# Block 0 of a fused attention and GEGLU kernel: other PSUM banks, an earlier third tile, two gates moved ahead

## The chip, the cores and the metric

The kernel runs on one core of a Trainium2 chip. The metric is the device time of one execution in microseconds; the value given for a kernel is the median of its runs. Before the change it is 328.77 us over 8 runs (328.52 to 329.89).

## What is computed

Two steps follow each other. A linear attention over 8 batches, 8 heads, 576 positions and 64 features per head; and a gated feed-forward layer on its output, seen as 4608 tokens of 512 channels, with 1536 hidden units. All tensors are float32 at the interface.

```python
r = np.maximum(x, 0.0)                        # phi of q and of k
phi = np.concatenate([r * cos_w, r * sin_w], axis=-1)
kv  = einsum('bhsf,bhsd->bhfd', phi(k), v)
num = einsum('bhsf,bhfd->bhsd', phi(q), kv)
den = einsum('bhsf,bhf->bhs', phi(q), sum_s phi(k)) + 1e-6
x   = (num / den)                             # tokens by 512 channels
g   = x @ w_gate
out = (0.5 * g * (1 + erf(g / sqrt(2))) * (x @ w_val)) @ w_out
```

## The kernel before, in words

**Work.** TensorE works in bfloat16. The tokens are cut into nine blocks: block 0 is batch 0 with its 576 tokens, and the others have 512 tokens, the last 448. A block's feed-forward part goes through the 12 groups of 128 hidden units, called `jt` in the code. `gate` (L212 to L222) multiplies one group's gate weights with the tokens in four accumulating matmuls into a PSUM bank, from which ScalarE writes the Gelu to a tile `gel`. `value` (L224 to L233) does the same with the value weights into another bank, and VectorE multiplies that bank by `gel` into `hT`. `gv_unit` is a gate and then its value. The output matmuls (L258) read `hT`.

**Banks.** One PSUM tile `ps` has 8 banks of 512 float32 columns, and every call names its bank as a number: the arguments of `gate` and `value` are block, group, first column, width and bank. Nothing is double-buffered by a pool here. A matmul into a bank waits until the last reader of that bank is done, so the numbers written in the calls decide who waits for whom. `gel` is from a rotating pool with 3 buffers.

**Order.** The order of instructions on every engine is the order of the Python calls (a manual schedule). Engines run in order, so a waiting instruction holds everything behind it on its engine.

**Block 0.** The start of the kernel cannot hide behind other work, so its calls are written out by hand (L396 to L439). The attention of batch 0 is cut into five tiles of tokens, the fifth with 64 tokens. For tile `t` these steps follow each other:

- `sq(t, which, engine)` (L134, L136) scales q by cosine or sine, on VectorE ("v") and ScalarE ("s").
- `q_by_pe(0, t, bank, engine)` (L323, L331, L333) transposes q in 8 matmuls and copies the bank to `qT`. `q_evac` is the copy alone.
- `Y(t, bank)` makes the numerators: 8 matmuls (L169), four into `bank` and four into `bank + 1`, then the division on VectorE (L181, L183, L184) into a tile `xb`.
- `X(t, bank, engine)` transposes `xb` in 4 matmuls (L342) into `bank`, and an engine copies it to `xT` (L345). Gates and values read `xT`.

As soon as a tile's columns of `xT` are there, gates and values on these columns can run. In block 0 the groups 0 and 1 are worked in pieces of 128 columns (0, 128, 256, 384) and a last one of 64 (512); later groups in A, 256 columns from 0, and Bw, 320 columns from 256. A loop (L467 to L472) then does the groups 4 to 11, with gate and value in the banks 0 and 3 for A and 1 and 2 for Bw, leaving out what the hand-written part has done.

**Queues.** The weights of the groups come by DMAs that GpSimd issues (L304, L305): groups 0 to 1, 2 to 3, 4 to 7 and later 8 to 11. Behind these in GpSimd's order stand the load of batch 1's q (L79), which may start when batch 0's q has been read, then the two halves of the output weights `wo_sb` (L443, L444), and a small copy (L445) that waits for the first half; the loads of batch 1's k and v on SyncE's queue wait for that copy.

**Dummies.** `dummies` (L123) issues matmuls on a zeroed tile `junk` at the start, while TensorE has nothing else to do.

Of the kernel before, what the change touches and what calls it, by code (L numbers as in the profile page):

```python
# [9 lines left out]
FP32 = mybir.dt.float32  # L10
BF16 = mybir.dt.bfloat16
# [5 lines left out]
def kernel(  # L17
# [31 lines left out]
    sb = ctx.enter_context(tc.tile_pool(name="sb", bufs=1))  # L49
    rot = ctx.enter_context(tc.tile_pool(name="rot", bufs=2))  # L50
# [16 lines left out]
    kv = [sb.tile([128, H, D + 2], BF16, name=f"kv{i}") for i in range(2)]  # L67

    hT = [sb.tile([128, JT, 64 + 576], BF16, name=f"hT{i}") for i in range(2)]
    ident = sb.tile([128, 128], BF16, name="ident")  # L70
    junk = sb.tile([128, 512], BF16, name="junk")
    tiny = sb.tile([1, 8], FP32, name="tiny")


# [54 lines left out]
    def scale(f, j, which, eng, h0=0, h1=H):  # L129
        dst, src = f  # L130
        col = (cos_c if which == 0 else sin_c)[:, j:j + 1]
        s, d = src[:, h0:h1, j, :], dst[:, j, h0:h1, which * D:(which + 1) * D]
        if eng == "v":
            nc.vector.tensor_scalar(d, s, col, 0.0, op0=ALU.mult, op1=ALU.max)  # L134
        else:
            nc.scalar.activation(d, s, AF.Relu, scale=col)  # L136
# [55 lines left out]
    def numer(b, t, bank, rows=128):  # L192

        numer_mm(b, t, bank, 0, rows)
        numer_mm(b, t, bank, 1, rows)
        xb = new_xb()
        norm(xb, bank, 0, 2, rows)
        return xb
# [12 lines left out]
    gels = {}  # L211

    def gate(n, jt, c0, w, gb):

        p0 = starts[n] + c0
        for ct in range(CT):
            nc.tensor.matmul(  # L217
                ps[:, gb, 0:w], lhsT=wg_sb[:, ct, jt * 128:(jt + 1) * 128],
                rhs=xT[:, ct, p0:p0 + w], start=(ct == 0), stop=(ct == CT - 1),
            )  # L220
        gels[n, jt, c0] = gel = rot.tile([128, 512], FP32, name="gel", bufs=3)
        nc.scalar.activation(gel[:, 0:w], ps[:, gb, 0:w], AF.Gelu)  # L222

    def value(n, jt, c0, w, vb):  # L224

        p0 = starts[n] + c0
        for ct in range(CT):
            nc.tensor.matmul(  # L228
                ps[:, vb, 0:w], lhsT=wv_sb[:, ct, jt * 128:(jt + 1) * 128],
                rhs=xT[:, ct, p0:p0 + w], start=(ct == 0), stop=(ct == CT - 1),  # L230
            )
        gel = gels.pop((n, jt, c0))
        nc.vector.tensor_mul(hT[n % 2][:, jt, 64 + c0:64 + c0 + w], gel[:, 0:w], ps[:, vb, 0:w])  # L233

    def gv_unit(n, jt, c0, w, gb, vb, mid=()):
        gate(n, jt, c0, w, gb)
        for f in mid:
            f()
        value(n, jt, c0, w, vb)
# [79 lines left out]
    def q_by_pe(b, j, bank, eng, h0=0, h1=H):  # L319

        qb = ps[:, bank, :].bitcast(BF16).rearrange("p (h t) -> p h t", h=H)
        for h in range(h0, h1):
            nc.tensor.transpose(out=qb[:, h, :], in_=qp[:, j, h, :], identity=ident)  # L323
        if eng is not None:
            q_evac(b, j, bank, eng, h0, h1)

    def q_evac(b, j, bank, eng, h0=0, h1=H):
        qb = ps[:, bank, :].bitcast(BF16).rearrange("p (h t) -> p h t", h=H)
        cp = nc.vector.tensor_copy if eng == "v" else nc.scalar.copy
        if j < NJ:  # L330
            cp(qT[b % 2][:, j, h0:h1], qb[:, h0:h1])  # L331
        else:
            cp(qT[b % 2][:, j, h0:h1, 0:64], qb[:, h0:h1, 0:128:2])  # L333

    def x_by_pe(b, t, xb, bank, eng, c0=0, c1=CT, every=1):
        p0 = b * S + t * 128
        cp = nc.vector.tensor_copy if eng == "v" else nc.scalar.copy
        xb2 = xb.rearrange("p g h d -> p (g h d)")
        rows = 128 if t < NJ or every == 2 else 64
        view = ps[:, bank, 0:256].bitcast(BF16).rearrange("p (c t) -> p c t", c=CT)  # L340
        for ct in range(c0, c1):
            nc.tensor.transpose(  # L342
                out=view[:, ct, 0:rows], in_=xb2[0:rows, ct * 128:(ct + 1) * 128], identity=ident[0:rows, 0:rows],
            )
        cp(xT[:, c0:c1, p0:p0 + rows // every], view[:, c0:c1, 0:rows:every])  # L345

    def sq(j, which, eng, *h):
        scale(Q, j, which, eng, *h)
# [48 lines left out]
    A, Bw = (0, 256), (256, 320)  # L397
    xs = {1: x1}

    def X(t, bank, eng):  # L400
        return lambda: x_by_pe(0, t, xs[t], bank, eng)

    def Y(t, bank):
        def f():
            xs[t] = numer(0, t, bank, 128 if t < NJ else 64)
        return f

    gate(0, 0, 0, 128, 5)
    gate(0, 1, 0, 128, 4)
    X(1, 2, "v")()  # L410
    q_evac(0, 2, 3, "v")
    sq(3, 0, "v"), sq(3, 1, "s")
    value(0, 0, 0, 128, 6)
    value(0, 1, 0, 128, 7)
    gate(0, 0, 128, 128, 5)
    gate(0, 1, 128, 128, 4)
    sq(4, 1, "s"), sq(4, 0, "v")
    value(0, 0, 128, 128, 6)
    value(0, 1, 128, 128, 7)
    Y(2, 2)()  # L420
    q_by_pe(0, 3, 0, "s")
    q_by_pe(0, 4, 1, "v")
    gv_unit(0, 2, *A, 4, 6)
    X(2, 0, "s")()
    Y(3, 2)()
    gv_unit(0, 3, *A, 5, 7)
    gv_unit(0, 0, 256, 128, 4, 6)
    X(3, 1, "v")()
    Y(4, 2)()
    gv_unit(0, 1, 256, 128, 5, 7)  # L430
    gv_unit(0, 0, 384, 128, 4, 6)
    gv_unit(0, 1, 384, 128, 5, 7)
    X(4, 0, "v")()
    gate(0, 4, *A, 3)
    gv_unit(0, 2, *Bw, 4, 6)
    gv_unit(0, 3, *Bw, 5, 7)
    value(0, 4, *A, 1)
    gv_unit(0, 0, 512, 64, 0, 2)
    gv_unit(0, 1, 512, 64, 4, 6)  # L439


    load_q(1, nc.gpsimd)
# [23 lines left out]
    }  # L466
    for jt in range(4, 12):  # L467
        for i, (c0, w) in enumerate((A, Bw)):
            if (jt, i) != (4, 0):
                gv_unit(0, jt, c0, w, i, 3 - i)  # L470
            for f in between.get((jt, i), ()):
                f()  # L472
# [52 lines left out]
    for n in range(1, 7):  # L525
# [6 lines left out]
        s = 0 if n > 1 else -1  # L532
# [68 lines left out]
```

## Time and profile before

| | |
|---|---|
| Median of 8 runs | 328.77 us |
| The profiled execution's own time | 328.52 us |
| Its span, first to last instruction | 326.4 us |
| Outside the span | 2.1 us |
| Mean granted TensorE clock | 1.000 |
| TensorE matmul busy | 316.7 us, 97% |
| VectorE busy | 172.2 us, 53% |
| ScalarE busy | 150.5 us, 46% |

In a profile line, L217 is line 217 of the kernel; PE is TensorE's matmuls, DVE is VectorE, ACT is ScalarE, POOL is GpSimd, SP is SyncE. A line of a timeline has the start, the time from the start to the end of the merged instructions, the engine, the line, the operation, `output<-inputs`, the shapes, the count, and in brackets how long the engine had been idle and what released it. Matmuls are pipelined: the next one starts well before the modelled end of the one before. So what a group of matmuls occupies is read from start to start, and an idle time in brackets, which counts from that modelled end, is shorter than the time that TensorE lost.

### The profile page before, as it was taken

What the parts mean: (1) busy time and instruction counts of PE and PEld (TensorE: products, weight loads), DVE (VectorE), ACT (ScalarE), POOL (GpSimd) and SP (SyncE); (2) the same over time, 40 slices, a digit from 0 to 9 for tenths busy, and PEclk for the clock granted to TensorE, in tenths of its full rate; (3) what the DMA queues carried; (4) which work ended last, traced back from release to release, by engine and by line L of the source; (5) the groups of instructions that cost most, each with busy time, mean ns of one, the idle gap of its engine ahead of it and who ended that gap; (6) DMA issues with size and microseconds to landing.
All of it is one profiled execution on the core that took longest, in us unless ns stands there. A gap on an engine that the chain in (4) does not pass through costs nothing.

```text
span 326.4 us, 5828 instructions
## 1 busy us (share of the span) xinstructions
PE 316.7 (97%) x2188; PEld 167.2 (51%) x2222; DVE 172.2 (53%) x383; ACT 150.5 (46%) x269; POOL 21.3 (7%) x41
## 2 busy tenths in 40 slices
PE   7999999999999999999999999999999999999994
PEld 3587866554445544544455445544554444444543
DVE  5895776868653667365835484548455222222210
ACT  6554664772483256425652375237622332323321
POOL 2640010000100010001000010001000100100000
PEclk9999999999999999999999999999999999999999
DMA  7999999896799929993799359994523211000024
GB/s 227 283 205 274 228 318 311 292 227 117 222 263 296 283 60 167 300 259 82 135 306 284 80 108 198 367 137 87 140 54 76 46 34 34 32 32 32 34 65 96
DMA packets 87739, 55.42 MB, mean 170 GB/s; under 512 B 52512, under 2 KB 82976, under 8 KB 87712
## 3 DMA queue, kind: packets, MB, share of 16 engines
q1 hardware_dynamic: 81200, 48.71, 59.7%
q0 software_dynamic: 6080, 5.90, 10.1%
q10 hardware_dynamic: 432, 0.46, 0.5%
q8 instruction: 17, 0.28, 0.4%
q14 instruction: 10, 0.08, 0.1%
HBM read 37.75 MB, written 9.44 MB: 145 GB/s over the span
## 4 chain that ended last, share of the span: by engine, by line
PE 94%; DVE 3%; issue 1%; ACT 0%; DVEq 0%
PE ps L217 28%; PE ps L258 28%; PE ps L228 27%; PE ps L169 3%; PE ps L153 3%; PE ps L126 2%; PE ps L323 1%; DVE hT L233 1%; PE ps L276 1%; PE ps L342 1%; DVE xb L184 1%; DVE vx L140 0%; DVE qp L134 0%; DVE rec L183 0%; DVE qT L331 0%
## 5 line engine op out<-in xcount | busy, mean ns | idle before, releaser
L233 DVE TENSOR_TENSOR hT<-gel,ps 128x512 bf16<-128x512 f32 (+5 forms) x126 | 76.4, 610 | 128.6 <-PE ps L228 121.8
L228 PE MATMUL ps<-xT,wv_sb 128*128 128x512 bf16 (+5 forms) x492 | 111.8, 348 | 1.1 <-DVE hT L233 0.8
L217 PE MATMUL ps<-xT,wg_sb 128*128 128x512 bf16 (+5 forms) x490 | 111.8, 348 | 1.0
L222 ACT ACTIVATE gel<-ps 128x512 f32<-128x512 f32 (+5 forms) x126 | 67.5, 536 | 77.6 <-PE ps L217 75.3
L258 PE MATMUL ps<-wo_sb,hT 128*128 128x512 bf16 x413 | 95.5, 379 | 0.6
L228 PEld LDWEIGHTS <-wv_sb 128*128 128x128 bf16 x504 | 47.9, 98 | 47.1 <-issue 1.0
L217 PEld LDWEIGHTS <-wg_sb 128*128 128x128 bf16 x504 | 45.7, 98 | 40.6 <-DVE xT L345 0.4
L258 PEld LDWEIGHTS <-hT 128*128 128x128 bf16 x420 | 40.1, 98 | 45.4
L287 ACT COPY o_sb<-ps 128x512 f32<-128x512 f32 x35 | 20.5, 585 | 75.4 <-PE ps L258 74.4
L184 DVE TENSOR_TENSOR xb<-ps,rec 128x512 bf16<-128x512 f32 (+2 forms) x41 | 27.8, 678 | 1.7 <-DVE rec L183 0.2
L136 ACT ACTIVATE kp<-kf,sin_c 128x512 bf16<-128x512 f32 (+1 forms) x41 | 25.4, 680 | 0.1
L134 DVE TENSOR_SCALAR qp<-qf,cos_c 128x512 bf16<-128x512 f32 x40 | 20.3, 547 | 0.0
L169 PEld LDWEIGHTS <-qT 128*128 128x128 bf16 (+1 forms) x320 | 15.0, 98 | 9.1 <-issue 2.3
L136 ACT ACTIVATE qp<-qf,sin_c 128x512 bf16<-128x512 f32 x28 | 19.3, 713 | 0.2 <-DMA qf<-in_q_dram 0.2
L134 DVE TENSOR_SCALAR kp<-kf,cos_c 128x512 bf16<-128x512 f32 (+1 forms) x45 | 18.6, 463 | 0.8 <-DMA kf<-in_k_dram 0.8
L169 PE MATMUL ps<-kv,qT 128*128 128x65 bf16 (+1 forms) x320 | 16.5, 193 | 0.5 <-DVE xb L184 0.3
L208 POOL COPY xT<-xr 128x256 bf16<-128x256 bf16 x6 | 2.4, 400 | 200.4 <-DMA xr<-xb 200.4
L153 PEld LDWEIGHTS <-kp 128*128 128x128 bf16 x320 | 10.9, 97 | 2.6 <-issue 0.7
L126 PE MATMUL ps<-junk 128*128 128x512 bf16 x33 | 10.1, 458 | 1.8 <-DVE par_i L103 1.7
L153 PE MATMUL ps<-vx,kp 128*128 128x65 bf16 x320 | 11.1, 193 | 0.1
L140 ACT CAST vx<-vf 128x1280 bf16<-128x1280 f32 (+1 forms) x9 | 9.7, 1075 | 1.2 <-DMA vf<-in_v_dram 1.2
L244 POOL COPY hT<-hT 128x768 bf16<-128x768 bf16 x8 | 7.6, 945 | 37.6 <-DVE hT L233 37.6
(55 smaller groups left out, 88.3 us busy)
## 6 DMA issues: line engine op xcount, KB each, us to landing
out_dram<-o_sb SPq DMA_DIRECT2D x38, 128.0 KB, 2.4
kf<-in_k_dram SPq DMA_DIRECT2D x7, 640.0 KB, 7.2
out_dram<-o_sb SPq DMA_DIRECT2D x16, 256.0 KB, 3.1
qf<-in_q_dram SPq DMA_DIRECT2D x6, 640.0 KB, 6.0
vf<-in_v_dram SPq DMA_DIRECT2D x6, 640.0 KB, 9.3
kf<-in_k_dram SPq DMA_DIRECT2D x7, 512.0 KB, 6.1
qf<-in_q_dram SPq DMA_DIRECT2D x6, 512.0 KB, 5.0
vf<-in_v_dram SPq DMA_DIRECT2D x6, 512.0 KB, 8.3
```

Of the source, the lines that this page charges most:

```text
L126: nc.tensor.matmul(ps[:, bank, :], lhsT=junk[:, 0:128], rhs=junk, start=True, stop=True)
L134: nc.vector.tensor_scalar(d, s, col, 0.0, op0=ALU.mult, op1=ALU.max)
L136: nc.scalar.activation(d, s, AF.Relu, scale=col)
L153: nc.tensor.matmul(ps[:, bank, (h % 4) * (D + 1):(h % 4 + 1) * (D + 1)], lhsT=kp[:, j, h, :], rhs=vx[b % 2][:, j, h, 0:D + 1], start=(j == ...
L169: nc.tensor.matmul(ps[0:rows, bank + g, (h % 4) * (D + 1):(h % 4 + 1) * (D + 1)], lhsT=qT[b % 2][:, t, h, 0:rows], rhs=kv[b % 2][:, h, 0:D ...
L184: nc.vector.tensor_tensor(xb[0:rows, g0:g1], nd[:, :, :, 0:D], rec[0:rows, 0:n, :, None].to_broadcast([rows, n, 4, D]), op=ALU.mult,)
L217: nc.tensor.matmul(ps[:, gb, 0:w], lhsT=wg_sb[:, ct, jt * 128:(jt + 1) * 128], rhs=xT[:, ct, p0:p0 + w], start=(ct == 0), stop=(ct == CT - 1),
L222: nc.scalar.activation(gel[:, 0:w], ps[:, gb, 0:w], AF.Gelu)
L228: nc.tensor.matmul(ps[:, vb, 0:w], lhsT=wv_sb[:, ct, jt * 128:(jt + 1) * 128], rhs=xT[:, ct, p0:p0 + w], start=(ct == 0), stop=(ct == CT - 1),
L233: nc.vector.tensor_mul(hT[n % 2][:, jt, 64 + c0:64 + c0 + w], gel[:, 0:w], ps[:, vb, 0:w])
L258: nc.tensor.matmul(ps[:, bank, :], lhsT=hT[n % 2][:, jt, c0:c0 + 128], rhs=wo_sb[:, jt, :], start=(jt == 0), stop=(jt == JT - 1),)
L287: nc.scalar.copy(o_sb, ps[:, bank, :])
```

## The change

The changed kernel keeps every computation; it reorders block 0, names other banks, and moves three copies between engines.

- **Tile of the dummies.** `junk` is no longer a tile of its own but the first 512 columns of group 0 in `hT[1]`, which is written for real in block 1.
- **Buffers.** `gel` has 4 buffers where it had 3.
- **First units.** The values of groups 0 and 1 on the columns 128 to 255 go to the banks 2 and 3 where they went to 6 and 7. The copy of `X(1, 2, ...)` goes from VectorE to ScalarE, that of `X(2, 0, ...)` from ScalarE to VectorE, that of the fourth tile from VectorE to ScalarE with bank 0 in place of 1, and the copy of the fifth tile's transposed q from VectorE to ScalarE.
- **Third tile.** `Y(2, 0)` stands right behind the first two values; it stood as `Y(2, 2)` behind the second two. All later `Y` use the banks 0 and 1.
- **Fifth tile of q.** `sq(4, ...)` and `q_by_pe(0, 4, ...)` come later.
- **Two gates ahead.** The gates of the groups 4 and 5 on A stand ahead of the last columns' units (before, that of group 4 alone), and their values behind them; the loop leaves out both.

```diff
+    junk = hT[1][:, 0, 0:512]
-    junk = sb.tile([128, 512], BF16, name="junk")
...
-        gels[n, jt, c0] = gel = rot.tile([128, 512], FP32, name="gel", bufs=3)
+        gels[n, jt, c0] = gel = rot.tile([128, 512], FP32, name="gel", bufs=4)
...
     gate(0, 0, 0, 128, 5)
     gate(0, 1, 0, 128, 4)
-    X(1, 2, "v")()
+    X(1, 2, "s")()
     q_evac(0, 2, 3, "v")
     sq(3, 0, "v"), sq(3, 1, "s")
     value(0, 0, 0, 128, 6)
     value(0, 1, 0, 128, 7)
+    Y(2, 0)()
     gate(0, 0, 128, 128, 5)
     gate(0, 1, 128, 128, 4)
+    value(0, 0, 128, 128, 2)
+    value(0, 1, 128, 128, 3)
+    q_by_pe(0, 3, 6, "s")
+    gate(0, 2, *A, 5)
+    X(2, 0, "v")()
     sq(4, 1, "s"), sq(4, 0, "v")
-    value(0, 0, 128, 128, 6)
-    value(0, 1, 128, 128, 7)
-    Y(2, 2)()
-    q_by_pe(0, 3, 0, "s")
-    q_by_pe(0, 4, 1, "v")
-    gv_unit(0, 2, *A, 4, 6)
-    X(2, 0, "s")()
-    Y(3, 2)()
-    gv_unit(0, 3, *A, 5, 7)
-    gv_unit(0, 0, 256, 128, 4, 6)
-    X(3, 1, "v")()
-    Y(4, 2)()
-    gv_unit(0, 1, 256, 128, 5, 7)
-    gv_unit(0, 0, 384, 128, 4, 6)
-    gv_unit(0, 1, 384, 128, 5, 7)
+    value(0, 2, *A, 7)
+    gate(0, 3, *A, 4)
+    Y(3, 0)()
+    value(0, 3, *A, 2)
+    q_by_pe(0, 4, 3, "s")
+    gv_unit(0, 0, 256, 128, 5, 6)
+    X(3, 0, "s")()
+    Y(4, 0)()
+    gv_unit(0, 1, 256, 128, 4, 7)
+    gv_unit(0, 0, 384, 128, 5, 2)
+    gv_unit(0, 1, 384, 128, 4, 3)
+    gate(0, 4, *A, 5)
     X(4, 0, "v")()
-    gate(0, 4, *A, 3)
-    gv_unit(0, 2, *Bw, 4, 6)
-    gv_unit(0, 3, *Bw, 5, 7)
-    value(0, 4, *A, 1)
-    gv_unit(0, 0, 512, 64, 0, 2)
-    gv_unit(0, 1, 512, 64, 4, 6)
+    gate(0, 5, *A, 4)
+    gv_unit(0, 2, *Bw, 1, 6)
+    gv_unit(0, 3, *Bw, 0, 7)
+    value(0, 4, *A, 3)
+    value(0, 5, *A, 2)
+    gv_unit(0, 0, 512, 64, 4, 6)
+    gv_unit(0, 1, 512, 64, 5, 7)
...
-            if (jt, i) != (4, 0):
+            if (jt, i) not in ((4, 0), (5, 0)):
                 gv_unit(0, jt, c0, w, i, 3 - i)
```

## The prediction

> **What bounds the kernel now.** First the page: engine shares and the chain of work that ended last.
>
> ```profile
> PE 316.7 (97%) x2188; PEld 167.2 (51%) x2222; DVE 172.2 (53%) x383; ACT 150.5 (46%) x269; POOL 21.3 (7%) x41
> ...
> PE 94%; DVE 3%; issue 1%; ACT 0%; DVEq 0%
> ```
>
> TensorE is busy 97% and makes 94% of the chain. The change keeps every matmul, so it can only win or lose TensorE's idle time in the stretch that it reorders, 16 to 31 us. Behind it, the list of TensorE's waits has one of 0.3 us after 60 us: what TensorE gains early is kept. Next, TensorE's timeline of the stretch.
>
> ```profile
> 16.27 0.61 PE L217 MATMUL ps<-xT,wg_sb 128*128 128x128 bf16 x8
> 16.85 0.40 PE L342 MATMUL ps<-ident,xb 128*128 128x128 bf16 x4
> 17.08 0.61 PE L228 MATMUL ps<-xT,wv_sb 128*128 128x128 bf16 x8
> 17.76 0.62 PE L217 MATMUL ps<-xT,wg_sb 128*128 128x128 bf16 x8
> 18.95 0.61 PE L228 MATMUL ps<-xT,wv_sb 128*128 128x128 bf16 x8 [0.56 <-DVE hT L233]
> 19.39 0.42 PE L169 MATMUL ps<-kv,qT 128*128 128x65 bf16 x8
> 19.65 1.05 PE L323 MATMUL ps<-ident,qp 128*128 128x128 bf16 x16
> 20.54 0.60 PE L217 MATMUL ps<-xT,wg_sb 128*128 128x256 bf16 x4
> 20.97 0.60 PE L228 MATMUL ps<-xT,wv_sb 128*128 128x256 bf16 x4
> ...
> 24.88 0.39 PE L217 MATMUL ps<-xT,wg_sb 128*128 128x128 bf16 x4
> 25.50 0.38 PE L228 MATMUL ps<-xT,wv_sb 128*128 128x128 bf16 x4 [0.23 <-DVE hT L233]
> ...
> 29.51 0.28 PE L228 MATMUL ps<-xT,wv_sb 128*128 128x64 bf16 x4
> 29.86 0.70 PE L217 MATMUL ps<-xT,wg_sb 128*128 128x320 bf16 x4
> ```
>
> Where nothing waits, the distance of starts gives what a matmul occupies: 16 transposes from 19.65 to 20.54, 0.056 us for 128 columns; likewise 0.109 for 256, 0.136 for 320, 0.029 for 64, and 0.033 in the numerators. A start later than that is lost time: 17.76 + 8 x 0.056 = 18.21, but the next row starts at 18.95. Last, hand-over times:
>
> ```profile
> 17.28 0.42 DVE L345 COPY xT<-ps 128x512 bf16<-128x512 bf16 x1 [0.49 <-PE ps L342]
> ...
> 20.29 1.01 ACT L331 COPY qT<-ps 128x1024 bf16<-128x1024 bf16 x1 [0.42 <-PE ps L323]
> ...
> 21.83 0.59 ACT L345 COPY xT<-ps 128x512 bf16<-128x512 bf16 x1 [0.24 <-PE ps L342]
> ```
>
> The first copy ends at 17.70 and TensorE starts at 17.76: 0.06 from engine to TensorE. The four transposes from 21.41 last 0.39 and ScalarE starts at 21.83: from the point where TensorE could go on (21.63) that is 0.16 for the pipeline and 0.04 for the hand-over. One copy of this size is 0.59 on ScalarE, 0.42 on VectorE.
>
> **What it removes.**
> - *Values on columns 128, banks 6 and 7.* Wait now 18.95 - 18.21 = 0.73: the bank is freed by a product that stands on VectorE behind the copies of xT and qT (17.28 to 18.30) and a scaling. The banks 2 and 3 are free by then. -0.73. Next late is nothing there; their products find VectorE free after the division.
> - *Value of group 1 on column 384, bank 7.* 24.88 + 0.22 = 25.10 against 25.50: 0.40. Its bank 3 was last read by the copy of the fifth q tile, which I place at 22.2 to 22.8. -0.40.
> - *First gate of the loop, bank 1.* 29.51 + 0.12 = 29.63 against 29.86: -0.24. Bank 1 is then last read by a Gelu some 2 us earlier.
> - *Gates on columns 128.* Wait now 17.08 + 0.45 = 17.53 to 17.76, 0.23. With ScalarE copying, xT comes at 17.28 + 0.59 + 0.06 = 17.93; the third tile's numerators (8 x 0.033) fill 17.53 to 17.79; 0.14 is left. -0.09. Their qT is ready: its copy, 0.68, now starts right after the division, at 16.7.
> - *Small ones.* Between the fourth tile's transposes and the fifth's numerators, which load 64 columns of weights, TensorE loses 0.09 (23.27 + 4 x 0.056 against 23.60); this falls inside a new wait. The last columns' first gate waits 0.05 for xT and will find it ready, with 0.44 of another gate ahead. Another 0.01 where the fourth tile's xb is awaited. Together -0.15.
>
> Sum removed: 0.73 + 0.40 + 0.24 + 0.09 + 0.15 = 1.61.
>
> **What it adds.** I carried every engine's new order forward with these durations. Applied to the old order, that gave TensorE's start at 32.91 within 0.02.
> - *The fifth tile's numerators now go to bank 0, into which the fourth tile has just been transposed.* TensorE must stand still for a whole copy: 0.16 + 0.04 + 0.59 + 0.06 = 0.85. No row shows this pair; the numerators write other columns and 64 partitions only. The built order has a wait on ScalarE at the first of them. [...] Everything on TensorE stands behind it. Upper end 1.1, were the copy of qT and a Gelu queued ahead on ScalarE to run late.
> - *Loop, group 5 on Bw.* Group 5 on A has gone, so groups 4 and 5 on Bw use the banks 1 and 2 in direct succession. The gate needs the Gelu (0.44, ScalarE row of 320 columns) done: 0.16 + 0.04 + 0.44 + 0.06 = 0.70 after the gate before, of which the value covers 0.54: 0.15. The value then waits for the product of 0.49 (VectorE row) with 0.11 in front: 0.82 - 0.70, 0.10 to 0.12. +0.25.
> - *The value of group 2 on A moves from 20.97 to 19.94.* Its weights, issued by GpSimd at 11.64, land 8.3 us later, and the last of the 16 parts is there at 19.99. +0.11 with the hand-over; between 0 and 0.4, since an earlier landing was never needed so exactly.
>
> Sum added: 0.85 + 0.25 + 0.11 = 1.21.
>
> **What costs nothing.** Group 5's gate and value on A (8 x 0.109 = 0.87) leave the loop and enter the hand-written part. The fourth `gel` buffer only removes ScalarE's waits (1.2 us there, which TensorE doesn't feel). The dummies read another zeroed address. Of the copies moved to ScalarE, the fifth q tile's gates nothing soon. The fifth q tile's scaling on ScalarE now comes behind a copy of 1.01 and a Gelu and ends near 21.43, not 19.87. Two things are queued on that: the transposes of q, which TensorE reaches at 21.6, cover 0.14; and GpSimd's second load of batch 1's q, issued now at 20.16 and then near 21.7, with both halves of `wo_sb` behind it (20.85, 21.66) 1.55 later. These land only 16 to 19 us after issue, because the queue ahead of them is full until 41; so I leave their landing. Were it 1.55 later, so would be batch 1's k, from 44.2 to 45.7, where ScalarE wants it at 45.55 - 0.40: 0.6 on ScalarE, of which the two output tiles (45.56 to 50.74; the features and v are ready at 50.16) cover all but 0 to 0.1.
>
> [...] By the row it is 1.61 - 1.21 = 0.40. [...]
>
> **Sum.** The profiled execution took 328.52 (span 326.4), 0.25 below the median of 328.77. 328.52 - 0.40 = 328.12 for it; for the median 328.77 - 0.40 = 328.37, so **328.4**. A measurement of this kernel tells about 0.2%, 0.66 us, from no change: bounds 328.11 and 329.43.
>
> **Rivals.**
> - *No new bank wait* (the numerators don't stand behind the copy): 0.40 + 0.85 = 1.25 gained, 327.5. For it: 64 partitions and other columns; against it: the wait in the built order. 0.10.
> - *ScalarE becomes the bound.* Three copies more, one less: 3 x 0.59 - 0.59 = 1.18 more in a stretch where it is 52% busy (7.86 of 15). The cover of 0.14 at the fifth q tile breaks and the copy under the numerators runs late: 0.3 to 0.5 lost, 328.8. 0.15.
> - *Slower: the weights of groups 2 and 3 land late.* The page's instruction queue q8 has 17 packets in 0.4% of 16 x 326.4 us, 1.2 us each. If one more sits ahead of the last part, it lands 1.2 later, TensorE stands 1.2 more at 19.94, and the time is 328.4 + 1.2 = 329.6. It turns to slower once the landing is more than 0.40 late, at 20.4. Against: the queue ahead of it isn't touched by the change. 0.07.
> - *The lead is lost again* at batch 1's loads, or the change does nothing in sum: 328.7. 0.08.
>
> The forecast has 0.60, range 328.0 to 328.7 (new bank wait 0.8 to 1.1, weights 0 to 0.4). With the rivals: **327.7 to 329.0**. Faster by over 0.2%: 0.10 and a fifth of the forecast, 0.22; slower: 0.07; within: 0.71.
>
> **What would show it.** In TensorE's timeline: the values on columns 128 follow their gates at once; a gap near 0.85 ahead of the 64-wide numerators, put down to ScalarE; about 0.1 ahead of the value of group 2; no gap at column 384; two small gaps at group 5 on Bw; the first output matmuls near 45.16, not 45.56. It is wrong if the gap at the numerators is missing or over 1.1, or if the output matmuls start early and the end does not follow.

## The result and the profile after

| | before | after |
|---|---|---|
| Median, us | 328.88 (328.52 to 329.89, 32 runs) | 327.82 (327.43 to 328.43, 12 runs) |
| Profiled execution's own time, its span, us | 328.52, 326.4 | 328.03, 325.9 |
| Mean granted TensorE clock | 1.000 | 1.000 |

The ratio is 0.9966, with a 95% interval of 0.9959 to 0.9974: the kernel became faster by 0.34% after this ratio and by 1.06 us after the medians, which is small but clear of noise. The forecast was 0.40 us. The median lies in the wide range of 327.7 to 329.0, but below the 328.0 to 328.7 that the forecast gave for its own account.

The page, engine shares and the chain of work that ended last, of the changed kernel (line numbers are one higher than before, up to the loop):

```profile
PE 316.4 (97%) x2188; PEld 167.1 (51%) x2222; DVE 171.0 (52%) x381; ACT 151.2 (46%) x271; POOL 21.3 (7%) x41
...
PE 93%; DMA 2%; DVE 1%; SPq 1%; issue 1%; POOL 0%; ACT 0%; POOLq 0%; DVEq 0%
```

TensorE still sets the time. One row that seemed to say nothing matters below: VectorE has 381 instructions in place of 383 and ScalarE 271 in place of 269, because the change moved four copies, not three: three went from VectorE to ScalarE and one the other way.

TensorE's timeline of the reordered stretch, after:

```profile
16.78 0.61 PE L218 MATMUL ps<-xT,wg_sb 128*128 128x128 bf16 x8
...
18.04 0.42 PE L170 MATMUL ps<-kv,qT 128*128 128x65 bf16 x8
18.43 0.61 PE L218 MATMUL ps<-xT,wg_sb 128*128 128x128 bf16 x8
18.88 0.61 PE L229 MATMUL ps<-xT,wv_sb 128*128 128x128 bf16 x8
...
22.95 0.40 PE L343 MATMUL ps<-ident,xb 128*128 128x128 bf16 x4
24.02 0.41 PE L170 MATMUL ps<-kv,qT 128*64 128x65 bf16 x8 [0.67 <-ACT xT L346]
24.36 0.40 PE L218 MATMUL ps<-xT,wg_sb 128*128 128x128 bf16 x4
...
25.27 0.39 PE L218 MATMUL ps<-xT,wg_sb 128*128 128x128 bf16 x4
25.49 0.39 PE L229 MATMUL ps<-xT,wv_sb 128*128 128x128 bf16 x4
...
30.31 0.28 PE L229 MATMUL ps<-xT,wv_sb 128*128 128x64 bf16 x4
30.43 0.71 PE L218 MATMUL ps<-xT,wg_sb 128*128 128x320 bf16 x4
30.97 0.71 PE L229 MATMUL ps<-xT,wv_sb 128*128 128x320 bf16 x4
31.66 0.70 PE L218 MATMUL ps<-xT,wg_sb 128*128 128x320 bf16 x4
32.33 0.70 PE L229 MATMUL ps<-xT,wv_sb 128*128 128x320 bf16 x4
```

Read as before, from start to start. The values on columns 128 follow their gates at once (18.43 + 0.45 = 18.88), so does the value of group 1 on column 384 (25.27 + 0.22 = 25.49), and so does the loop's first gate (30.31 + 0.12 = 30.43). Ahead of the 64-wide numerators there is a hole. The four transposes before them, the first 0.067 and the others 0.056 each, occupy TensorE until 22.95 + 0.23 = 23.18. The numerators start at 24.02, 0.84 later, with ScalarE's copy of `xT` named as the releaser. This is the copy:

```profile
23.38 0.58 ACT L346 COPY xT<-ps 128x512 bf16<-128x512 bf16 x1
```

**Where the time came from.** The first gate starts at 16.27 us in this execution of before and at 16.78 in this one of after. That is not the change: over the eleven profiled executions of this study it lies between 16.07 and 16.84, also for kernels that are the same up to there, and it goes with the landing of the first loads: the fourth load of k landed at 6.79 where the gate started at 16.07, at 6.93 in before, and at 7.52 in after. So each trace is cut at marks behind it. The first two lie at the gates above (16.27 and 16.78) and at the first output matmul, here before and then after:

```profile
45.56 5.34 PE L258 MATMUL ps<-wo_sb,hT 128*128 128x512 bf16 x23
```

```profile
45.52 0.81 PE L259 MATMUL ps<-wo_sb,hT 128*128 128x512 bf16 x2
```

| | before | after | gain |
|---|---|---|---|
| Stretch: first gate to the first output matmul | 29.29 | 28.73 | 0.56 |
| Middle: the third matmul of one value in block 1, near 61 us, to the start of the last matmul | 260.62 | 260.40 | 0.22 |
| End: start of the last matmul to the end of the span | 4.63 | 4.40 | 0.23 |

The sum is 1.01 us; the medians give 1.06. Almost half of it (0.22 + 0.23 = 0.45) comes from places that the change does not touch. The changed kernel run again shows the same parts within 0.01, below.

### The profile page after: what moved, and what is told of

Its sections match the earlier page's. It is cut to its first block, busy times and chain, and to the rows that moved or that the text cites. A ratio compares the mean times of both kernels' runs of the same rounds, so it can differ in the third digit from the quotient of the medians.

```text
span 325.9 us, 5830 instructions
## 1 busy us (share of the span) xinstructions
PE 316.4 (97%) x2188; PEld 167.1 (51%) x2222; DVE 171.0 (52%) x381; ACT 151.2 (46%) x271; POOL 21.3 (7%) x41
## 4 chain that ended last, share of the span: by engine, by line
PE 93%; DMA 2%; DVE 1%; SPq 1%; issue 1%; POOL 0%; ACT 0%; POOLq 0%; DVEq 0%
PE ps L218 28%; PE ps L229 28%; PE ps L259 28%; PE ps L170 3%; PE ps L154 3%; DMA vf<-in_v_dram 2%; SPq L80 1%; PE ps L277 1%; PE ps L324 1%; PE ps L343 1%; DVE xb L185 0%; DVE hT L234 0%; DVE vx L141 0%; DVE rec L184 0%; ACT xT L346 0%
## 5 line engine op out<-in xcount | busy, mean ns | idle before, releaser
L127 PE MATMUL ps<-hT 128*128 128x512 bf16 x33 | 10.1, 459 | 1.8 <-DVE par_i L104 1.7
```

The lines of the kernel that those rows point to most:

```text
L127: nc.tensor.matmul(ps[:, bank, :], lhsT=junk[:, 0:128], rhs=junk, start=True, stop=True)
```

## The experiments

Two theories stood against each other. **By terms:** the reordering's own terms were mis-sized, or the two edits put down at nothing bring something. **By position:** the reordering gave about what was forecast, and the rest comes from VectorE having two instructions fewer, which moves all its later instructions by two places in its stream. The second theory was read from the traces of experiments 1 to 4; experiments 5 to 9 were forecast and built with it in view.

Every kernel was timed beside the kernel before, on the same chip. "Stretch", "middle" and "end" are the three parts of the table above.

**1. The changed kernel again**, and **2. the kernel before with the two edits that were put down at nothing.**

```diff
 (2, against before)
+    junk = hT[1][:, 0, 0:512]
-    junk = sb.tile([128, 512], BF16, name="junk")
...
-        ... name="gel", bufs=3)
+        ... name="gel", bufs=4)
```

> The changed kernel once more, for a second profile. It gained 1.06 us in the median (328.88 to 327.82), but its profile shows only 0.56 won in the reordered stretch. Theory A (the reordering wins 0.56, and the rest is won later, because some waits behind 60 us no longer occur): the stretch from the first gate to the first output matmul is again about 28.7 us (before 29.3), and time is also won between 60 and 150 us. Theory B (the first profile of before or after is not typical): ahead of the first gate the start is near 16.3 us, not 16.8, the stretch is about 28.8, and between 60 us and the end the two kernels take the same time within 0.1. Time near 327.8 in both.

> The kernel before with only the parts of the change that reorder nothing: gel with 4 buffers, and the dummies on the tile hT[1]. Theory A1 (the fourth buffer takes waits away in the later blocks, where ScalarE waited for VectorE's product): 0.3 to 0.5 us of the gain, so 328.4. Theory B (these parts cost and bring nothing; my prediction): 328.9, the same as before within 0.2.

Measured: the changed kernel 327.83 against 328.80 for before, ratio 0.9973 (0.9963 to 0.9983); stretch 28.74, middle 260.41, end 4.39. With the two edits alone 328.76, ratio 1.0000 (0.9991 to 1.0009); parts 29.30, 260.61 and 4.64. The gain repeats, and the fourth `gel` buffer and the other address of the dummies have no part in it.

**3. Other banks for the values on columns 128, in the old order.** The change's largest single term was 0.73 us for these.

```diff
 (against before)
-    value(0, 0, 128, 128, 6)
-    value(0, 1, 128, 128, 7)
+    value(0, 0, 128, 128, 0)
+    value(0, 1, 128, 128, 1)
     Y(2, 2)()
-    q_by_pe(0, 3, 0, "s")
-    q_by_pe(0, 4, 1, "v")
+    q_by_pe(0, 3, 6, "s")
+    q_by_pe(0, 4, 7, "v")
```

> The kernel before with only the banks changed for the first units: the values of groups 0 and 1 on columns 128 go to the banks 0 and 1, the transposes of the fourth and fifth q tiles to 6 and 7; no call is moved. My prediction booked 0.73 us for this wait alone. If that term stands by itself: 328.2. The rival: with the order unchanged TensorE comes to the fifth q tile at about 19.4 and its scaling on ScalarE ends only at 19.87, so 0.53 of wait comes up there, and another 0.04 at the value behind; the stretch wins only 0.1 and the time is 328.8.

Measured: 328.82, ratio 1.0002 (0.9993 to 1.0011); stretch 29.15, 0.14 shorter. TensorE's timeline of this kernel:

```profile
18.02 0.61 PE L228 MATMUL ps<-xT,wv_sb 128*128 128x128 bf16 x8
18.47 0.42 PE L169 MATMUL ps<-kv,qT 128*128 128x65 bf16 x8
18.75 0.61 PE L323 MATMUL ps<-ident,qp 128*128 128x128 bf16 x8
19.73 0.62 PE L323 MATMUL ps<-ident,qp 128*128 128x128 bf16 x8 [0.38 <-DVE hT L233]
```

The wait of 0.73 is gone, but soon after TensorE arrives too early at the transposes of the fifth q tile: 18.75 + 8 x 0.056 = 19.20, and they start at 19.73, 0.53 lost. The bracket names a product on VectorE that ends at about the same time, but these transposes neither read it nor write its bank. What they read is the q tile that ScalarE has just scaled:

```profile
18.96 0.71 ACT L136 ACTIVATE qp<-qf,sin_c 128x512 bf16<-128x512 f32 x1
```

It ends at 19.67, and 0.06 more for the hand-over is 19.73. So in the old order the bank numbers alone are worth 0.14, and the fifth q tile takes the rest back. The change puts that tile later, and the forecast's "next late is nothing there" holds for the whole change, not for this edit.

**4. A free bank for the fourth tile's transposes.** It removes what the forecast called the price of the change, the pair of transposes and numerators in bank 0.

```diff
 (against after)
-    X(3, 0, "s")()
+    X(3, 7, "s")()
```

> The changed kernel with the fourth tile's transposes and copy in bank 7, not in bank 0, so that the fifth tile's numerators need not wait for the copy. If the wait of 0.84 us ahead of them is the bank's, as I read it: it falls to about 0.1 (then the fifth q tile's copy on ScalarE ends last), a new wait of about 0.13 comes ahead of the value of group 1 on column 256, which uses bank 7, and the time falls by 0.6 to 327.2. If something else held the numerators (the q copy on ScalarE): the gap stays at 0.6 or more and the time at 327.7.

Measured: 327.02, ratio 0.9945 (0.9933 to 0.9958); stretch 28.15, middle 260.04, end 4.39. TensorE's timeline of this kernel:

```profile
22.87 0.40 PE L343 MATMUL ps<-ident,xb 128*128 128x128 bf16 x4
23.21 0.44 PE L170 MATMUL ps<-kv,qT 128*64 128x65 bf16 x8
23.58 0.40 PE L218 MATMUL ps<-xT,wg_sb 128*128 128x128 bf16 x4
23.94 0.38 PE L229 MATMUL ps<-xT,wv_sb 128*128 128x128 bf16 x4
```

The numerators now start 0.34 behind the transposes, not 1.07. That shows the shared bank as the cause of 0.73 of the 0.84. The remaining 0.10 has nothing to do with the bank: the kernel before has 0.09 at the same place. Of the 0.73 won, 0.13 is given back ahead of the next value, whose bank 7 is now the one being read (23.94 in place of 23.58 + 0.23 = 23.81): 0.59 remains. The middle, though, became 0.36 shorter, which nothing in this edit explains. VectorE has one record fewer in this trace (574 in place of 575); the next pair takes that up.

**5. and 6. VectorE's position by itself.** VectorE's records in a trace were counted from 0, waits and drains among them (before has 577, after 575). A wait is a record of its own. An instruction right behind it that nothing else holds starts 0.04 us after it in the median; but if it falls on number 191, 319, 447 or 575, every 128th, it starts 0.40 to 0.47 after it, in every trace, be it a product, a division or a drain. If such a number falls on an instruction in a back-to-back run, nothing is seen: in after, 191 is a reciprocal and starts 0.035 behind its forerunner, like any other. (Number 63 is no test: in after it is a copy that waits longer by itself, in before a reciprocal in a run, 0.11 behind its forerunner.) Two kernels move the numbering and nothing else, with tiny writes to a scratch tile in block 0.

```diff
 (5, against after: two fillers; 6, against before: ten)
+    pad = sb.tile([1, 8], FP32, name="pad")
+    for _ in range(2):
+        nc.vector.memset(pad, 0.0)
```

> The changed kernel with two one-row memsets added on VectorE at about 30 us, where VectorE idles; nothing waits for them. Counted in VectorE's records of an execution, a delay of about 0.4 us comes at every 128th (numbers 191, 319, 447, 575 in the kernel before), wherever that record falls; the change took two records out of VectorE's stream ahead of them (577 before, 575 after). Theory C (0.2 us of the gain behind 60 us and 0.24 us in the tail come only from that shift): with 577 records again the time from 61 us to the last matmul goes from 260.4 back to 260.6, the time behind the last matmul from 4.39 back to 4.63, and the whole from 327.83 to 328.3, while the reordered stretch stays at 28.7. Theory A (these gains belong to the reordering or to the fourth buffer): 327.8 and no such shift.

> The kernel before with ten one-row memsets added on VectorE at about 30 us, and nothing else: more work, no less waiting in block 0. Theory C: the delayed records now fall ten places earlier in the program, on instructions with slack (a copy of v or a scaling ahead of the product at 69 us; a product at 136; a reciprocal at 209; a product at 311), so that the waits of TensorE at 73 and 142 us vanish (late part 260.6 to about 260.1) and the tail shortens from 4.63 to 4.39: 328.8 to 328.1, faster by adding instructions. Theory A: 328.8 or a little slower.

Measured: after with two fillers 328.50, ratio 0.9987 (0.9978 to 0.9995), parts 28.74, 260.62 and 4.61. Before with ten fillers **327.95, ratio 0.9971 (0.9960 to 0.9983)**, parts 29.30, 260.05 and 4.39. Ten more instructions make the kernel before 0.9 us faster, with its stretch unchanged; two more take from the changed kernel what it had won behind 60 us (0.21 and 0.22 of its 0.22 and 0.23). Here is how it looks. VectorE's timeline near 72 us, before and then before with ten fillers:

```profile
72.05 0.69 DVE L233 TENSOR_TENSOR hT<-gel,ps 128x512 bf16<-128x512 f32 x1 [2.24 <-PE ps L169]
```

```profile
71.77 0.69 DVE L233 TENSOR_TENSOR hT<-gel,ps 128x512 bf16<-128x512 f32 x1 [1.85 <-PE ps L228]
```

It is the same product. In before it is record 191, and VectorE has been idle for 2.24; with fillers it is number 201, and the idle time is 1.85, 0.39 less. (It reads the value's bank and needs L228 in both; L169 is only what had come last before the late start.) What TensorE makes of it, again before and then with fillers:

```profile
72.74 0.81 PE L228 MATMUL ps<-xT,wv_sb 128*128 128x512 bf16 x3
73.83 0.41 PE L169 MATMUL ps<-kv,qT 128*128 128x65 bf16 x8 [0.28 <-DVE xb L184]
```

```profile
72.83 0.81 PE L228 MATMUL ps<-xT,wv_sb 128*128 128x512 bf16 x3
73.55 0.42 PE L169 MATMUL ps<-kv,qT 128*128 128x65 bf16 x8
```

From the same matmul of the value to the numerators 1.09 us pass in before and 0.72 with fillers: 0.37 lost to a division that the late product has held up. The rest of before's middle, 260.62 - 260.05 - 0.37 = 0.20, falls to record 319, a division:

```profile
141.72 0.69 DVE L184 TENSOR_TENSOR xb<-ps,rec 128x512 bf16<-128x512 f32 x1 [0.23 <-DVE rec L183]
```

TensorE's numerators behind it come 1.12 after their value starts (141.34 to 142.46), and 0.93 with fillers (141.06 to 141.99), 0.19 apart.

The changed kernel pays too, but less. Its record 191 is harmless, as said, and its record 319 is a product, behind which TensorE waits once. Here is that product, then TensorE in after, then TensorE in before with ten fillers:

```profile
142.42 0.69 DVE L234 TENSOR_TENSOR hT<-gel,ps 128x512 bf16<-128x512 f32 x1 [0.61 <-PE ps L170]
```

```profile
142.97 1.03 PE L229 MATMUL ps<-xT,wv_sb 128*128 128x512 bf16 x4
144.19 0.41 PE L170 MATMUL ps<-kv,qT 128*128 128x65 bf16 x8 [0.20 <-DVE xb L185]
```

```profile
143.10 1.03 PE L228 MATMUL ps<-xT,wv_sb 128*128 128x512 bf16 x4
143.97 0.42 PE L169 MATMUL ps<-kv,qT 128*128 128x65 bf16 x8
```

That is 1.22 against 0.87, 0.35 lost, and 260.05 + 0.35 = 260.40, the middle of after. So before pays 0.57 in the middle and after 0.35: this is the whole gain of 0.22 there. All eleven traces sort by the number of their records alone: 577 gives a middle of 260.61 to 260.63, 575 gives 260.40 or 260.41, and 574, 576 and 587 give 260.04 to 260.06. In experiment 4 (574 records) number 319 falls into a run, which explains its 0.36.

Record 575 is the drain that closes the kernel: it starts 0.47 behind its wait in before; in after the same drain is record 573 and starts 0.09 behind it. That is the "end".

What makes these records late no run shows. One thing in the traces goes with their numbers. The page's instruction queue q14 moves 10 packets with 0.08 MB in before, 8 KB each. The list of DMA queues in the window from 66 to 71 us has none of them in before, and one with fillers:

```profile
q1 hardware_dynamic: 3888, 0.99, 110.3%
```

```profile
q1 hardware_dynamic: 4042, 1.03, 115.4%
q14 instruction: 1, 0.01, 0.5%
```

In before this packet comes at 74.78, 2.7 behind record 191, and with ten fillers at 68.31, 2.4 behind it. The one behind record 319 moves alike, from 145.72 to 139.79, and with fillers, where record 575 is a product at 310.13, one comes at 311.34, where before has none. (The queue brings other packets too, one at 98.72 and one at 98.62, one at 310.44 and one at 309.96; these do not move with the fillers.) So a packet follows these records by 1 to 4 us and goes with the number, not with the time.

**7. Third tile's numerators later**, behind the values on columns 128, as in before.

```diff
 (against after)
     value(0, 1, 0, 128, 7)
-    Y(2, 0)()
     gate(0, 0, 128, 128, 5)
     gate(0, 1, 128, 128, 4)
     value(0, 0, 128, 128, 2)
     value(0, 1, 128, 128, 3)
+    Y(2, 0)()
```

> The changed kernel with one call moved back: the third tile's numerators stand behind the second two values again. By the forward reckoning that made my prediction, the gates on columns 128 then wait 0.40 for ScalarE's copy (0.14 with the numerators in between) and the third tile's transposes wait about 0.5 for the division, so the stretch grows by 0.6 to 29.35 us: 328.4 to 328.5. If the early numerators do not matter: 327.8.

Measured: 328.77 against 328.87, ratio 0.9996 (0.9988 to 1.0005); stretch 29.53, middle 260.41, end 4.40. The stretch is 0.80 longer than in after and even 0.24 longer than in before. TensorE's timeline of this kernel:

```profile
17.29 0.61 PE L229 MATMUL ps<-xT,wv_sb 128*128 128x128 bf16 x8
18.13 0.61 PE L218 MATMUL ps<-xT,wg_sb 128*128 128x128 bf16 x8 [0.23 <-ACT xT L346]
...
19.72 0.60 PE L218 MATMUL ps<-xT,wg_sb 128*128 128x256 bf16 x4
20.68 0.40 PE L343 MATMUL ps<-ident,xb 128*128 128x128 bf16 x4 [0.35 <-DVE xb L185]
```

Two waits appear: 18.13 - 17.29 - 0.45 = 0.39 ahead of the gates on columns 128, which nothing covers now while ScalarE copies, and 20.68 - 19.72 - 0.44 = 0.52 ahead of the third tile's transposes, whose division starts later. The kernel has 575 records like after, and its middle and end are the same, so the numbering has no part in this. The place of `Y(2, 0)` carries the gain of the stretch: without it the change would have lost there.

**8. One gate ahead, not two.** Group 5 on A goes back into the loop.

```diff
 (against after)
-    gate(0, 5, *A, 4)
...
-    value(0, 5, *A, 2)
...
-            if (jt, i) not in ((4, 0), (5, 0)):
+            if (jt, i) != (4, 0):
```

> The changed kernel with group 5 on A back in the loop, so that one gate stands ahead of the last columns, not two. Reckoned: the last columns' first gate waits about 0.54 for the fifth tile's copy, the two waits for banks at group 5 on Bw (0.15 and 0.12) vanish, 0.2 more in sum: stretch 28.95, time 328.0. If the second gate ahead brings nothing but its bank clash: the stretch shrinks by 0.27.

Measured: 327.73, ratio 0.9967 (0.9955 to 0.9979); stretch 29.07, middle 260.05, end 4.42. By its time this gate is worth nothing. By its parts it is: without it TensorE waits for the last columns' `xT`,

```profile
25.95 0.29 PE L343 MATMUL ps<-ident,xb 64*128 64x64 bf16 x4
26.62 0.70 PE L218 MATMUL ps<-xT,wg_sb 128*128 128x320 bf16 x4 [0.38 <-DVE xT L346]
```

26.62 - 25.95 - 0.12 = 0.55 lost, and the stretch is 0.34 longer. But VectorE's numbering shifted by one (576 records), number 319 falls on a wait, and the middle is 0.36 shorter. The two cancel. This execution also shows the wait for weights ahead of the value of group 2 that the forecast put at 0.11:

```profile
19.78 0.39 PE L343 MATMUL ps<-ident,xb 128*128 128x128 bf16 x4
20.12 0.61 PE L229 MATMUL ps<-xT,wv_sb 128*128 128x256 bf16 x4
```

It is 20.12 - 19.78 - 0.22 = 0.12 here; the last of these weights landed at 20.08.

**9. What the runs point to**, together: the free bank of 4, the next two values' banks exchanged, and the loop's banks alternating so that groups 4 and 5 on Bw no longer follow each other in the same two banks.

```diff
 (against after)
-    X(3, 0, "s")()
+    X(3, 7, "s")()
...
-    gv_unit(0, 1, 256, 128, 4, 7)
+    gv_unit(0, 1, 256, 128, 4, 3)
...
-    gv_unit(0, 1, 384, 128, 4, 3)
+    gv_unit(0, 1, 384, 128, 4, 7)
...
-                gv_unit(0, jt, c0, w, i, 3 - i)
+                par = (i + (jt > 4)) % 2 if (jt, i) != (5, 1) else 0
+                gv_unit(0, jt, c0, w, par, 3 - par)
```

> The changed kernel with the fourth tile's transposes in bank 7 (as in free_bank), the value of group 1 on column 256 in bank 3 and that on column 384 in bank 7, and the loop's banks alternating also across the units that it leaves out. By the reckoning the 0.13 ahead of the value on column 256 and the 0.15 and 0.13 at group 5 on Bw vanish: stretch 27.75 (free_bank 28.15), time 326.6 if no delayed record of VectorE falls on a product or on the tail, up to 0.45 more if one does.

Measured: **326.48** against 328.94, ratio 0.9924 (0.9911 to 0.9938); stretch 27.76, middle 260.04, end 4.42. It beats both kernels, and the bank waits ahead of the fifth tile's numerators, of the value behind them and at group 5 on Bw are gone. Of the 1.34 us below after, 0.97 are in the stretch; 0.36 in the middle are again the numbering (574 records), not the banks. TensorE's timeline of this kernel:

```profile
23.21 0.40 PE L218 MATMUL ps<-xT,wg_sb 128*128 128x128 bf16 x4
23.44 0.39 PE L229 MATMUL ps<-xT,wv_sb 128*128 128x128 bf16 x4
...
29.27 0.71 PE L218 MATMUL ps<-xT,wg_sb 128*128 128x320 bf16 x4
29.81 0.71 PE L229 MATMUL ps<-xT,wv_sb 128*128 128x320 bf16 x4
30.36 0.71 PE L218 MATMUL ps<-xT,wg_sb 128*128 128x320 bf16 x4
```

The value now follows its gate by 0.23, where experiment 4 had 0.36, and the second gate on Bw follows the first value by 0.55, where after had 0.69. Against experiment 4 the stretch became 28.15 - 27.76 = 0.39 shorter: 0.13 at the value, and the remaining 0.26 at the loop, which is the forecast's +0.25 measured by removing it.

## Why the prediction was right, and where its size was wrong

The mechanism in block 0 was right, nearly step by step. The size was not: 1.06 in place of 0.40. The step that failed is the sentence that the change "can only win or lose TensorE's idle time in the stretch that it reorders". What TensorE gained early was kept, but the time behind the stretch was put at no change, and it changed by 0.45. The one wait of 0.3 us after 60 us that the forecast read and passed over was the trace of it: it is the wait at 73.83, behind record 191. That the median still lies in the range of 327.7 to 329.0 is luck. Below 328.0 the range was widened for rivals, and the only one on that side, the one without a bank wait, did not come about; the forecast's own 328.0 to 328.7 was missed.

- *Values on columns 128, -0.73; value of group 1 on column 384, -0.40; loop's first gate, -0.24.* All three waits are gone from the timeline. Experiment 3 shows that, in the old order, the first is not had by bank numbers alone.
- *Gates on columns 128.* Forecast 0.14 left, measured 18.43 - 18.04 - 8 x 0.033 = 0.13.
- *Fifth tile's numerators, +0.85.* Measured 0.84, of which 0.10 is there without the shared bank. Experiment 4 shows the wait by taking the sharing away. The program itself holds this wait; what the chip would do without it no run shows. The rival without this wait, 327.5, is excluded, though the median lies nearer to it than to the forecast. That nearness is an accident, because the added 0.45 has another source.
- *Group 5 on Bw, 0.15 and 0.10 to 0.12.* Measured 31.66 - 30.97 - 0.54 = 0.15 and 32.33 - 31.66 - 0.54 = 0.13. Right.
- *Value of group 2 waiting for weights, +0.11.* Not there in the profiled execution of after, where these weights had landed at 19.89 and TensorE came to them at 20.43. It is 0.12 in experiment 8, where they landed at 20.08. It depends on the landing in the execution at hand.
- *Sum of the stretch.* Forecast 0.40, or 0.51 without the wait for weights; measured 0.56. The first output matmuls stand at 45.52, not at the forecast 45.16: the start of this execution was 0.51 late, and 45.52 - 0.51 = 45.01.
- *0.056 for a matmul of 128 columns.* The values on columns 128 follow their 8 gates after 0.45, 0.056 each, again.
- *ScalarE becomes the bound.* It did not: the copy under the numerators ran at 23.38, 0.20 behind the transposes' 23.18, as fast as the forecast's 0.16 + 0.04. *Weights 1.2 us late* and *the lead lost again* did not happen either.
- *Moved copies.* The forecast asked what a copy costs ScalarE and what it spares VectorE. It did not ask which of VectorE's later instructions get which number. That was worth 0.22 in the middle and 0.23 at the end, 0.45 in all, more than the forecast gain of the whole change. At equal numbering (experiment 5) the change is worth 0.37 us by the medians, with an interval of 0.16 to 0.72, and 0.55 in its stretch.

Still open: why every 128th record can start late. The 8 KB packets on q14 go with the numbers of these records, 1 to 4 us behind them, but that they have to do with the delay no run shows.

## What to carry to other kernels

Ask of every unit pulled ahead which bank it writes and who read that bank last: in this change one shared bank cost 0.73 us and its renaming gave 0.59 back. Price a removed wait by the next late thing on the same engine, since a wait of 0.73 was worth 0.14 alone. And before a gain or loss below 1 us in a kernel of 330 is put down to an edit, compare the traces behind the edited stretch and repeat the kernel with a few fillers: here two instructions more or less on a half-idle engine moved the later parts of the trace by 0.43 to 0.45 us.

## What the runs showed of the hardware that was not expected

- On VectorE every 128th record of the trace (191, 319, 447, 575) starts 0.35 to 0.43 us late if it stands right behind a wait, and on time inside a back-to-back run. It cost 0.37 (record 191 in before), 0.35 (319 in after) or 0.20 (319 in before) where TensorE waited for that result, 0.23 as the closing drain, and nothing elsewhere (record 447 in before, a product at 212.32). A packet of 8 KB on the page's instruction queue q14 follows within 1 to 4 us (74.78 behind record 191 at 72.05 in before, 311.34 behind record 575 at 310.13 with ten fillers).
- The first gate starts between 16.07 and 16.84 us with the same instructions ahead of it, and goes with the landing of the first loads (6.79 to 7.52 us for the fourth of k). Behind that point the parts of the changed kernel, profiled twice, repeat within 0.01 us, so traces of this kernel are best compared from there.
